# Clustered attention with a gated convolution FFN: the first batch's slots in another order, and every engine's order list written anew

## Chip, cores and metric

The kernel runs on one core of one Trainium2 chip. The metric is the device time of one execution in microseconds (us), median over several runs. The core's engines each work through their own instructions in order: PE multiplies matrices, DVE and POOL do vector work, ACT does activations (exp, relu, tanh, copies), and SP issues transfers; they wait for each other by semaphores.

## The reference

Four batches, 8 heads, 768 tokens, head size 64. Each query and key is assigned to one of 16 centroids of its head; a query sees only the keys of its own cluster. The attention output, 512 wide, goes through an FFN with a depthwise convolution of three taps over the tokens and a sigmoid gate. Cut to what matters:

```python
q_assign = argmax(einsum('bhsd,hcd->bhsc', q_n, c_n), -1)      # the same for k
scores = where(q_assign[..., :, None] == k_assign[..., None, :], q @ k.T / 8, -1e9)
attn = exp(scores - max); attn /= sum(attn) + 1e-9
x = (attn @ v)                      # heads side by side: 4 x 768 x 512
h = maximum(x @ w_in, 0)            # 1024 wide
conv = sum_k conv_w[k] * h shifted by k - 1 tokens
out = (h * sigmoid(conv)) @ w_out   # 4 x 768 x 512, float32
```

## The kernel before

**Tiling.** The heads go in pairs: 4 pairs per batch, 16 pairs in all, numbered g. A pair's queries are cut into two halves of 384. One pair and one half of the queries make a *slot* t: 8 slots per batch, 32 in all. `slot(t)` gives the pair and the half of a slot; for the first batch from the table `SLOTS0`, for the others half by half, pair by pair. In the table before, slots 0 to 3 are the first half of pairs 0 to 3 and slots 4 to 7 their second half.

**One pair is prepared** so: q and k come in by DMA (`L`, `LQ`, `LK`, `LZ`), are transposed on PE (`T`, line 309) and copied from PSUM (`Qa` by ACT, line 315, `Qd` by DVE, line 317), or transposed in blocks on DVE (`Z`, line 298); half precision copies go into `ext` (`CD` on POOL, `CDd` on DVE, `CDa` on ACT, lines 321 and 323). PE multiplies them with the centroids (`A`, line 347), DVE finds the largest in seven steps (`M0` to `M6`, lines 364 to 389). The cluster number is coded into three extra rows of `ext`, so that the product of q and k gets the mask with it: PE turns the codes (`K` and `B`, and `BX` writes the rows by DMA; or `KM` on PE and `KCa`/`KCd` copy them straight from PSUM; `BA` is `BX` on ACT's DMA queue). The rows of `ext` that are not used are zeroed once (`_z` on POOL, `_zd` on DVE, line 716). There are six `ext` buffers.

**One slot** has six steps i: `S.t.i` multiplies two key tiles with the 384 queries (line 442, contracting over all 128 rows of `ext`), `E.t.i` takes the exp of both on ACT (line 454). `V.t.u` multiplies with v (line 466; v loaded by `LV`, cast by `CV`), `N.t` divides by the sums on DVE, and x is transposed into `xT` by PE (`X`, then `Ya`/`Yd`) or by DMA (`XD`).

**The FFN** of a batch works on a half of the tokens: it needs the `xT` of all four pairs of that half. `I.n.f` multiplies with w_in (line 524), `Ra`/`Rd` is the relu (ACT line 537, DVE line 539), `C` carries the tokens at the border between the halves, `a`, `b`, `c` are the three taps on DVE (lines 558, 560) or `W` the same as matmuls on PE, `H` the tanh, `G` the gate on DVE, `O`/`U` multiply with w_out (line 604), `Fa`/`Fd` take the result out of PSUM and `FX` stores it. Weights come in pieces (`_wl`), cast by POOL, DVE or ACT (`_wp`, `_wd`, `_wa`); `_tp`, `_td`, `_ta` build the diagonal matrices of the taps; `_k` runs three matmuls on zeros.

**The order** of all this is written out by hand: `PLAN` is a list of such tokens. They are issued in this order, and each engine, and SP's queue of transfers, keeps the order in which its own instructions come up. Two things share buffers in turn: four input buffers hold the q and k of the pairs and also the pieces of weights (`load_weights` uses the tag `qk_in`), and the PSUM banks, whose number stands behind `@` in a token. A line of the list begins with the exp that opens a slot (`E.t.0`).

Of the kernel before, what the change touches and what calls it, by code (L numbers as in the profile page):

```python
# [155 lines left out]
def kernel(  # L156
# [12 lines left out]
    B, H, S, D = q.shape  # L169
    P = 128  # L170
    J = S // P
    C = 16
# [3 lines left out]
    R = Dm // P  # L176
    HS = S // 2
    VW = D + 2
    NPR = H // 2
    SPB = 2 * NPR  # L180
    NU = 2 * NPR
    BR = 3
    SHARP = 24.0


    CUT = HS - 2
    LO = (0, CUT)
    NCV = (CUT, S - CUT)
# [31 lines left out]
    NE = 6  # L220
# [216 lines left out]
    def scores(t, i):  # L437
        b, a, pr, g = slot(t)
# [433 lines left out]
```

## Time and profile before

| | us |
|---|---|
| median of 3 runs | 241.73 (241.42 to 241.91) |
| the profiled execution, its own time | 240.68 |
| its span | 238.9 |
| matmuls busy (PE) | 227.7 |
| DVE busy | 215.4 |
| ACT busy | 215.4 |
| POOL busy | 84.6 |
| the exps on ACT, 192 of them | 146.4 |

The span is what the hardware profiler records between the first and the last instruction; the execution's own time has what lies around it too. Busy times of engines overlap; a busy PE means that some matmul was in flight. The granted TensorE clock was 0.998 of full speed over the span.

### The profile page before, as it was taken

How to read it: one execution, taken by the hardware profiler on the slowest of the kernel's cores; microseconds unless marked ns; L12 is line 12 of the kernel's file. 1: busy time of each engine (PE TensorE's matmuls, PEld its weight loads, DVE VectorE, ACT ScalarE, POOL GpSimd, SP SyncE). 2: the span in 40 equal slices, each digit the busy share in tenths (PEclk: the TensorE clock that was granted, in tenths of full speed). 3: DMA queues.
4: the chain of work that ended last, by engine and by line, in shares of the span. 5: the costliest groups of instructions: out<-in, count | busy, mean ns of one | idle time of the engine just before them, and what ended most of it. 6: DMA issues, size and time to landing. Idle time of an engine off the chain costs nothing.

```text
span 238.9 us, 6438 instructions
## 1 busy us (share of the span) xinstructions
PE 227.7 (95%) x2442; PEld 143.5 (60%) x2442; DVE 215.4 (90%) x497; ACT 215.4 (90%) x337; POOL 84.6 (35%) x149
## 2 busy tenths in 40 slices
PE   7988998999999999999999999999999999999984
PEld 4665665575556566655666666655776666555531
DVE  6999999989999999999899999999899999983850
ACT  5998997999999999999999999999999999994542
POOL 8559664790168335411935031304540001000000
PEclk9999999999999999999999999999999999999999
DMA  7988599944956975878669507890542110323104
GB/s 198 294 243 257 157 233 245 323 80 83 242 92 136 183 128 94 173 126 183 163 150 169 114 3 188 153 134 1 168 89 63 33 47 16 105 64 112 68 0 177
DMA packets 102958, 32.77 MB, mean 137 GB/s; under 512 B 94603, under 2 KB 98187, under 8 KB 102926
## 3 DMA queue, kind: packets, MB, share of 16 engines
q1 hardware_dynamic: 102599, 32.11, 57.3%
q8 instruction: 19, 0.31, 0.6%
q10 hardware_dynamic: 327, 0.24, 0.4%
q14 instruction: 13, 0.11, 0.1%
HBM read 23.11 MB, written 6.29 MB: 123 GB/s over the span
## 4 chain that ended last, share of the span: by engine, by line
PE 64%; DVE 15%; ACT 12%; POOL 5%; issue 2%; DVEq 0%; POOLq 0%
PE sc L442 17%; PE flex L524 15%; PE flex L604 14%; PE flex L466 10%; ACT attn L454 8%; PE flex L347 3%; POOL ext L323 3%; PE sc L566 3%; ACT th L584 2%; DVE best L380 1%; DVE ext L323 1%; DVE cnv L560 1%; DVE x L480 1%; PE sc L604 1%; DVE val L377 1%
## 5 line engine op out<-in xcount | busy, mean ns | idle before, releaser
L454 ACT ACTIVATE attn<-sc 128x768 f16<-128x768 f32 x192 | 146.4, 817 | 4.0 <-PE sc L442 2.7
L442 PE MATMUL sc<-ext 128*128 128x384 f16 x384 | 89.3, 325 | 3.8 <-ACT attn L454 2.1
L466 PEld LDWEIGHTS <-attn 128*128 128x128 f16 x1152 | 50.5, 97 | 15.2 <-ACT attn L454 0.4
L560 DVE SCALAR_TENSOR_TENSOR cnv<-hpad,cwcol,cnv 128x382 f16<-128x382 f16 (+1 forms) x100 | 58.4, 609 | 0.4
L323 POOL CAST ext<-qkT 64x768 f16<-64x768 f32 x48 | 41.7, 875 | 40.6 <-DVE qkT L298 20.0
L466 PE MATMUL flex<-v,attn 128*128 128x65 f16 x1152 | 54.5, 193 | 0.3 <-ACT attn L454 0.3
L524 PE MATMUL flex<-xT,w_in 128*128 128x384 f16 x256 | 49.1, 326 | 0.1
L442 PEld LDWEIGHTS <-ext 128*128 128x128 f16 x384 | 32.5, 97 | 26.9 <-issue 9.2
L604 PE MATMUL flex<-w_out,hg 128*128 128x512 f16 x176 | 47.1, 379 | 0.0
L592 DVE SCALAR_TENSOR_TENSOR hg<-th,hpad 128x764 f16<-128x764 f32 (+2 forms) x33 | 30.7, 934 | 3.1 <-ACT th L584 3.0
L524 PEld LDWEIGHTS <-w_in 128*128 128x128 f16 x256 | 23.9, 98 | 15.6 <-issue 0.6
L604 PEld LDWEIGHTS <-hg 128*128 128x128 f16 x192 | 17.9, 98 | 16.8 <-DVE hg L592 1.1
L537 ACT ACTIVATE hpad<-flex 128x384 f16<-128x384 f32 x45 | 21.8, 501 | 2.4 <-PE flex L524 1.6
L323 POOL CAST v<-v_in 128x768 f16<-128x768 f32 x15 | 14.6, 977 | 24.7 <-DMA v_in<-in_v_dram 24.6
L584 ACT ACTIVATE th<-cnv 128x764 f32<-128x764 f16 (+1 forms) x25 | 21.2, 848 | 0.7 <-DVE cnv L560 0.7
L323 POOL COPY hpad<-hf 128x6 f16<-128x6 f16 x12 | 4.9, 418 | 42.0 <-DVE hg L592 41.8
L480 DVE TENSOR_TENSOR x<-flex,rec 128x384 f16<-128x384 f32 x32 | 17.8, 558 | 1.1
L298 DVE STREAM_TRANSPOSE qkT<-qk_in 128x768 f32<-128x768 f32 x18 | 17.3, 966 | 0.0
L558 DVE TENSOR_SCALAR cnv<-hpad,cwcol 128x382 f16<-128x382 f16 (+1 forms) x50 | 16.3, 349 | 0.6 <-ACT hpad L537 0.5
L323 POOL COPY hf<-hpad 128x6 f16<-128x6 f16 x11 | 3.6, 329 | 30.7 <-ACT hpad L537 18.6
L347 PE MATMUL flex<-qkT,cT 128*32 128x192 f32 x256 | 14.1, 333 | 0.0
L309 PE MATMUL flex<-id,qk_in 128*128 128x128 f32 x84 | 12.5, 287 | 1.2 <-ACT qkT L315 0.6
(82 smaller groups left out, 217.1 us busy)
## 6 DMA issues: line engine op xcount, KB each, us to landing
v_in<-in_v_dram SPq DMA_DIRECT2D x16, 384.0 KB
out_dram<-o_sb SPq DMA_DIRECT2D x24, 256.0 KB
qk_in<-in_q_dram SPq DMA_DIRECT2D x36, 96.0 KB
qk_in<-in_k_dram SPq DMA_DIRECT2D x36, 96.0 KB
qk_in<-in_q_dram SPq DMA_DIRECT2D x5, 384.0 KB
qk_in<-in_k_dram SPq DMA_DIRECT2D x5, 384.0 KB
w_sb<-in_moe_w_out_dram SPq DMA_DIRECT2D x2, 768.0 KB
w_sb<-in_moe_w_in_dram SPq DMA_DIRECT2D x3, 512.0 KB
```

The lines of the kernel that those rows point to most:

```text
L323: (nc.vector if name == "d" else nc.gpsimd).tensor_copy(out=to, in_=src)
L347: nc.tensor.matmul(bank[at][32 * j : 32 * (j + 1), 192 * i : 192 * (i + 1)], lhsT=cT32[:, which, :], rhs=tokens[:, j], start=True, stop=Tr ...
L442: nc.tensor.matmul(s[:, n, 0:HS], lhsT=ext_b[g % NE][:, h, 1, P * (kt + n) : P * (kt + n + 1)], rhs=ext_b[g % NE][:, h, 0, HS * a : HS * ( ...
L454: nc.scalar.activation(attn[t, i // 3][:, kt : kt + 2, :], sc[(6 * t + i) % 2][:, :, 0:HS], AF.Exp, scale=0.125)
L466: nc.tensor.matmul(avp(at)[:, u, 0 : D + 1], lhsT=attn[t, h][:, kt, P * jq : P * (jq + 1)], rhs=v16_b[g % NE][:, h, kt, 0 : D + 1], start= ...
L480: nc.vector.tensor_tensor(out=x16[t].rearrange("p jq (h d) -> p h jq d", h=2), in0=av[:, :, 0:D].rearrange("p (h jq) d -> p h jq d", h=2), ...
L524: nc.tensor.matmul(bank[at][:, 0:HS], lhsT=w_in16[:, r, 2 * u + f, :], rhs=xT[:, b % 2, r, HS * a : HS * (a + 1)], start=(r == 0), stop=(r ...
L537: nc.scalar.activation(to, src, AF.Relu)
L560: nc.vector.scalar_tensor_tensor(out=cnv, in0=src, scalar=w, in1=cnv, op0=ALU.mult, op1=ALU.add)
L584: nc.scalar.activation(th_t[n][:, fs, 0:N], pre[:, fs, 0:N], AF.Tanh, scale=0.5)
L592: nc.vector.scalar_tensor_tensor(out=hg_b[b][:, 2 * u + fs.start : 2 * u + fs.stop, LO[a] : LO[a] + N], in0=th_t[n][:, fs, 0:N], scalar=1. ...
L604: nc.tensor.matmul(bank[at][:, 0:Dm], lhsT=hg_b[b][:, fb, P * tq : P * (tq + 1)], rhs=w_out16[:, fb, :], start=(fb == 0), stop=(fb == NFB ...
```

## The change

Three edits. The table `SLOTS0` gets another order: slot 0 is the first half of pair 0 as before, slot 1 is the second half of the same pair, and then come the first halves of pairs 1, 2 and 3 and the second halves of pairs 1, 2 and 3. `PLAN` is written anew as a whole: the order of the tokens in all slots, the PSUM banks, and for some small steps the engine that does them (relus, casts, copies, taps, memsets); transfers of bias rows for pair 1, head 1 move from ACT's queue (`BA.1.1`) to SP's (`BX.1.1`); one group of matmuls on zeros (`_k.3`) is left out. The matmuls of the scores name their rows by a constant `KR`, which is 128.

The diff, with the list's first slots and its end:

```diff
-    "LQ.0.0 _id _io _zero _k.10@2 _zd.5.0 _k.17@3 _zd.3.0 _zd.3.1 _pk.4 _sd _z.0.1 _k.14@1 _hz.1 _z.1.1 "
-    "_cent _n1 _z.1.0 _z.0.0 _hz.2 _pk.0 _v.1 _z.2.1 _pk.2 _pk.1 _z.4.0 T.0.0@2 La.0.0 T.0.1@1 _n0 _nq _n2 "
-    "_n5 _id16 _zd.4.1 _n3@3 _n4@3 Qa.0.0 Qa.0.1 CDd.0.0.1 CDa.0.0.0 LK.0.1 T.0.3@2 Qa.0.3 A.0.0@3 M0.0.0 "
-    "M1.0.0 M2.0.0 M3.0.0 _cw0 LQ.0.1 T.0.2@1 Qa.0.2 CDa.0.1.1 LQ.1.0 T.1.0@0 _cw1@2 _cw2 _tp.20 Qa.1.0 "
-    "A.0.1@1 M4.0.0 M0.0.1 M1.0.1 M5.0.0 M2.0.1 M6.0.0 M3.0.1 LK.1.0 T.1.1@3 Qa.1.1 _ta.10 CDd.1.0.0 LQ.1.1 "
-    "T.1.2@1 Qa.1.2 LK.1.1 T.1.3@0 A.1.0@2 M0.1.0 M1.1.0 Qa.1.3 CD.1.1.1 _ta.6 _td.22 KM.0.0.1@1 KCa.0.0.1 "
-    "KM.0.0.0@3 KCd.0.0.0 M4.0.1 M2.1.0 M3.1.0 M4.1.0 A.1.1@2 M0.1.1 M5.1.0 M5.0.1 M6.1.0 M6.0.1 M1.1.1 "
-    "_z.5.1 CDa.0.1.0 S.0.0 "
-    "E.0.0 L.2 T.2.0@0 Qa.2.0 T.2.2@1 Qa.2.2 T.2.1@3 Qa.2.1 CD.2.1.1 CD.1.1.0 CD.1.0.1 S.0.1 E.0.1 _n7d "
...
-    "S.0.3 E.0.3 S.0.4 E.0.4 K.1.1@0 B.1.1 BA.1.1 _ta.7 M4.2 M5.2 M6.2 L.4 T.4.2@3 T.4.0@2 T.4.1@1 S.0.5 "
...
-    "S.4.0 T.6.1@0 Qd.6.1 V.2.5@2 K.5@3 S.4.1 "
...
-    "V.5.5@2 N.5 CD.7.0.1 CD.6.1.0 _wl.1 _wp.4 _wp.3 _wl.2 _wp.6 _v.5 I.0.0@0 Rd.0.0 c.0.0 _wa.7 _wa.5 "
...
+    "_sd _pk.4 _zero _k.10@2 _zd.4.1 _k.17@3 _k.14@3 _pk.3 _id _id16 _z.0.1 _pk.1 _z.0.0 _pk.0 _z.1.0 _io "
+    "_z.2.1 _z.1.1 _v.2 LQ.0.0 T.0.0@3 _cent _n1 _zd.5.1 La.0.0 _n0 _nq _n2 _n3@1 _n5 _n4@1 Qa.0.0 T.0.1@2 "
+    "Qd.0.1 CDd.0.0.1 LK.0.1 T.0.3@0 LQ.0.1 T.0.2@3 Qa.0.2 Qa.0.3 CDa.0.1.0 CD.0.1.1 A.0.0@1 M0.0.0 M1.0.0 "
+    "LQ.1.0 _cw0 _cw1@3 _cw2 _ta.10 _tp.11 A.0.1@2 M2.0.0 LK.1.0 LK.1.1 T.1.3@3 T.1.0@0 _z.3.1 M0.0.1 M3.0.0 "
+    "M1.0.1 M4.0.0 M2.0.1 LQ.1.1 T.1.2@2 Qa.1.0 Qa.1.2 T.1.1@1 Qa.1.1 M5.0.0 M6.0.0 M3.0.1 M4.0.1 KM.0.0.1@2 "
+    "KCd.0.0.1 Qa.1.3 _ta.9 CDa.0.0.0 CD.1.1.1 CD.1.0.0 _z.2.0 _n7d A.1.0@1 M0.1.0 M1.1.0 M2.1.0 KM.0.0.0@3 "
+    "KCa.0.0.0 _ta.23 A.1.1@2 M0.1.1 L.2 T.2.0@0 Qa.2.0 S.0.0 "
+    "E.0.0 S.0.1 T.2.1@3 Qa.2.1 T.2.2@2 Qa.2.2 S.0.2 M3.1.0 M4.1.0 M5.1.0 M5.0.1 M6.0.1 _tp.20 _v.4 M1.1.1 "
+    "M2.1.1 M6.1.0 CD.2.1.1 M3.1.1 M4.1.1 CD.1.1.0 CD.1.0.1 CD.2.0.0 CD.2.0.1 KM.0.1.0@1 K.1.0@3 B.1.0 "
+    "KCd.0.1.0 A.2@2 M0.2 KM.0.1.1@3 KCd.0.1.1 _v.1 M1.2 M2.2 E.0.1 CDa.2.1.0 E.0.2 _ta.19 L.3 T.3.0@0 "
+    "Qa.3.0 T.3.2@2 Qd.3.2 T.3.1@3 Qa.3.1 CD.3.0.1 _v.0 S.0.3 S.0.4 E.0.3 E.0.4 CD.3.1.0 _tp.15 M5.1.1 M3.2 "
+    "M4.2 M5.2 M6.1.1 A.3@2 M0.3 M6.2 CDa.3.1.1 S.0.5 E.0.5 S.1.0 "
+    "E.1.0 M1.3 K.1.1@2 B.1.1 L.4 T.4.2@0 T.4.0@3 Qa.4.0 _ta.4 T.4.1@1 Qd.4.2 Qd.4.1 L.5 LV.0 BX.1.0 S.1.1 "
+    "S.1.2 CD.3.0.0 CV.0 _pk.2 E.1.1 L.6 LV.1 BX.1.1 T.5.0@2 Qa.5.0 M2.3 M3.3 CDd.4.0.1 K.2@0 B.2 LV.2 A.4@3 "
...
+    "S.3.3 K.4@2 S.3.4 V.2.0@1 V.2.1@1 E.3.3 E.3.4 S.3.5 E.3.5 _wl.4 _wd.14 V.2.2@1 V.2.3@1 M2.5 V.2.4@1 "
+    "V.2.5@1 N.2 M3.5 BX.3 S.4.0 _wl.0 LV.3 LZ.7.0 LZ.7.1 S.4.1 "
...
+    "E.5.0 _wd.0 V.3.5@3 N.3 S.5.2 M2.6 V.4.3@1 V.4.4@1 E.5.1 E.5.2 S.5.3 E.5.3 V.4.5@1 X.2@0 Ya.2 N.4 "
+    "V.5.0@2 V.5.1@2 S.5.4 S.5.5 _hz.2 CD.6.0.0 _tp.6 _wp.13 CD.6.1.0 _z.5.0 _wp.12 CD.6.1.1 E.5.4 _ta.8 "
+    "E.5.5 M3.6 M4.6 A.7@3 M0.7 _wd.1 M1.7 S.6.0 V.5.2@2 K.5@0 S.6.1 "
+    "E.6.0 V.5.3@2 V.5.4@2 E.6.1 S.6.2 E.6.2 M5.6 M6.6 CDa.7.1.1 _wl.1 _wl.2 _wd.8 BX.4 X.3@1 K.6@3 B.6 B.5 "
+    "Yd.3 V.5.5@2 N.5 S.6.3 E.6.3 S.6.4 E.6.4 CD.7.0.0 CD.7.0.1 M2.7 _wp.4 _tp.18 _wp.5 _wp.6 XD.4 I.0.1@3 "
+    "I.0.0@2 Rd.0.0 c.0.0 M3.7 Ra.0.1 c.0.1 a.0.0 a.0.1 b.0.0 b.0.1 _wp.3 _wp.7 LV.5 CV.5 S.6.5 E.6.5 "
...
+    "U.3.3.4@5 H.31.0 H.31.1 G.31.0 G.31.1 U.3.3.5@5 U.3.3.6@5 U.3.5.0@3 U.3.3.7@5 U.3.5.1@3 U.3.5.2@3 "
+    "U.3.2.6@4 Fa.3.3 FX.3.3 U.3.5.3@3 U.3.2.7@4 U.3.5.4@3 U.3.5.5@3 U.3.5.6@3 U.3.5.7@3 Fa.3.2 FX.3.2 "
...
+    KR = P
...
-    SLOTS0 = ((0, 0), (0, 1), (0, 2), (0, 3), (1, 0), (1, 1), (1, 2), (1, 3))
+    SLOTS0 = ((0, 0), (1, 0), (0, 1), (0, 2), (0, 3), (1, 1), (1, 2), (1, 3))
...
-                lhsT=ext_b[g % NE][:, h, 1, P * (kt + n) : P * (kt + n + 1)],
-                rhs=ext_b[g % NE][:, h, 0, HS * a : HS * (a + 1)],
+                lhsT=ext_b[g % NE][0:KR, h, 1, P * (kt + n) : P * (kt + n + 1)],
+                rhs=ext_b[g % NE][0:KR, h, 0, HS * a : HS * (a + 1)],
```

232 rows, old and new, of the table PLAN are left out of this document.

## The prediction

> **What bounds the kernel now.** I read the page's totals first, then the windows that cut the span where the stages change, then what ACT waited for, then the order of time around those waits. The first fence is from the page: the span and the busy time of each engine.
>
> ```profile
> span 238.9 us, 6438 instructions
> PE 227.7 (95%) x2442; PEld 143.5 (60%) x2442; DVE 215.4 (90%) x497; ACT 215.4 (90%) x337; POOL 84.6 (35%) x149
> ```
>
> Three engines are at 90% or more, so no single total says which one ends the program. The windows do: busy time of PE, PEld, DVE, ACT and POOL (and how many instructions) before the first exp, from there to the last exp of slot 10, to the end of the last exp, and the tail.
>
> ```profile
> 0.00:13.52 13.52, 10.92 (x90) 7.03 (x91) 11.15 (x32) 10.41 (x20) 9.10 (x36) 1.00 0.94 249
> 13.52:79.22 65.70, 61.64 (x765) 41.18 (x764) 62.69 (x156) 62.41 (x97) 38.35 (x57) 1.00 0.77 190
> 79.22:215.74 136.52, 136.26 (x1477) 85.70 (x1476) 131.55 (x293) 133.23 (x205) 36.95 (x55) 1.00 0.52 108
> 215.74:238.90 23.16, 18.86 (x116) 9.61 (x113) 9.97 (x19) 9.35 (x17) 0.19 (x1) 0.98 0.25 92
> ```
>
> From 79.22 to 215.74 us PE has 0.26 us without a matmul: there PE is the bound, ACT and DVE are close behind, and the same PE work in another order takes about the same time. Between 13.52 and 79.22 us PE lacks 4.06 us, ACT 3.29 us and DVE 3.01 us: no engine is full, they wait for each other. A change to the first batch can win there, and before it in the head, where ACT is idle for 3.11 us.
>
> What ACT waited for between 5 and 80 us (total, times, longest), and those two places in the order of time (start, length, engine, instruction, idle before it):
>
> ```profile
> ACT attn L454 <- PE sc L442: 1.6, 3, 1.2
> ACT taps L745 <- DVE pack L389: 0.9, 1, 0.9
> ```
>
> ```profile
> 21.22 1.37 ACTq L410 DMA_DIRECT2D ext<-spk  x1
> 22.64 0.40 ACT L745 ACTIVATE taps<-id,cwcol 128x128 f16<-128x128 f16 x1 [0.93 <-DVE pack L389]
> ...
> 40.53 0.22 PE L401 MATMUL flex<-id,pack 128*128 128x128 f16 x1 [0.43 <-DVE qkT L317]
> ...
> 41.11 2.41 ACT L454 ACTIVATE attn<-sc 128x768 f16<-128x768 f32 x3 [1.23 <-PE sc L442]
> ```
>
> The first place: ACT stands 0.93 us while its own queue issues the bias rows' DMA of pair 1, head 1 (`BA.1.1`, 1.37 us). The second: in slot 4 the order list puts `K.5@3` ahead of `S.4.1`, so a turn that waits for DVE holds up the scores, and ACT loses 1.23 us.
>
> **The change, part by part.** `KR = P` leaves both operands of the scores as they are: nothing. The slots' order and the lists are the change. With slot 1 on pair 0, pair 1 is first needed in slot 2, pairs 2 and 3 in slots 3 and 4, one slot later than now; the first half's FFN input needs slots 0, 2, 3, 4. Counted in the two lists, every matrix product, exp, argmax, gate and store is there once in both; what differs is who does the small work. Durations are the group means (busy us, then mean ns of one):
>
> ```profile
> L537 ACT ACTIVATE hpad<-flex 128x384 f16<-128x384 f32 x45 | 21.8, 501 | 2.4 <-PE flex L524 1.6 <-DVE hg L592 0.2
> L321 ACT ACTIVATE ext<-flex 3x768 f16<-3x768 f16 x2 | 1.6, 801 | 0.1
> L321 ACT ACTIVATE w_in<-w_sb 128x512 f16<-128x512 f32 x2 | 1.1, 620 | 0.0
> L745 ACT ACTIVATE taps<-id,cwcol 128x128 f16<-128x128 f16 x9 | 3.5, 402 | 0.9 <-DVE pack L389 0.9
> L323 DVE CAST ext<-qkT 64x768 f16<-64x768 f32 x9 | 5.5, 610 | 0.2
> L539 DVE TENSOR_SCALAR hpad<-flex 128x384 f16<-128x384 f32 x19 | 10.4, 549 | 1.7 <-PE flex L524 1.7
> L748 DVE TENSOR_SCALAR taps<-id,cwcol 128x128 f16<-128x128 f16 x5 | 1.6, 321 | 0.0
> L716 DVE MEMSET ext<- 64x768 f32 x4 | 2.8, 698 | 0.6 <-issue 0.4
> L323 POOL CAST ext<-qkT 64x768 f16<-64x768 f32 x48 | 41.7, 875 | 40.6 <-DVE qkT L298 20.0 <-PE sc L442 11.3 <-ACT qkT L315 4.5
> L323 POOL CAST v<-v_in 128x768 f16<-128x768 f32 x15 | 14.6, 977 | 24.7 <-DMA v_in<-in_v_dram 24.6
> L748 POOL TENSOR_SCALAR taps<-id,cwcol 128x128 f16<-128x128 f16 x10 | 6.9, 694 | 1.6 <-DVE cwcol L734 1.1
> L716 POOL MEMSET ext<- 64x768 f32 x8 | 5.7, 733 | 0.3
> ```
>
> DVE: 3 relus fewer (-1.65), 3 casts of ext fewer (-1.83), 4 taps fewer (-1.28), 2 memsets fewer (-1.40): -6.2 us, of which about 1.8 us comes back (two casts of v and one copy of bias rows, priced like ext casts at 0.610). Net -4.3 us, 1.4 of it in the head; single small steps that go either way are left out. POOL takes it: 3 ext casts (+2.63), 5 taps (+3.47), 2 memsets (+1.47), 2 v casts fewer (-1.95): +5.6 us. ACT up to the last exp of slot 10: one copy of bias rows fewer (-0.80), two weight casts fewer (-1.24), one relu more (+0.50), one tap more (+0.40): -1.1 us. PE: three warm-up matmuls fewer in slot 0; they lie in the stage in which PE lacks 4.06 us of work, so they are hidden there and I price them at nothing (if PE were short of time, their going would be a gain).
>
> *Up to slot 10.* ACT has 62.41 of 65.70 us filled, so 1.1 us less work on it shows as 1.1 us: **-1.1** (0 if it only adds idle time; -1.1). `BA.1.1` becomes `BX.1.1` on SP: the 0.93 us stall goes: **-0.9** (0 to -0.93). What it now stands behind is SP's loads. Counted in the list, pairs 0 to 6 and two values, 6.3 MB, go out ahead of it; the head's rate is
>
> ```profile
> DMA packets 9440, 4.16 MB, mean 260 GB/s; under 512 B 8047, under 2 KB 9436, under 8 KB 9439
> ```
>
> so it lands near 6.3 / 0.26 = 24 us or shortly after its own issue, and `S.2.3` wants it only at about 30: hidden, and if not, 1 us for each us it is late. The stall before `S.4.1`: in the new list no turn lies between `S.3.5` and `S.4.1`, but what DVE does late can hold another token. Bounds -1.23 and 0; I take half: **-0.6**.
>
> *The head* pays. These rows are the present chain to the first exp:
>
> ```profile
> 5.48 0.70 DVE L716 MEMSET ext<- 64x768 f32 x1 [0.20 <-issue]
> 6.78 0.53 PE L347 MATMUL flex<-qkT,cT 128*32 128x192 f32 x8
> 7.24 0.87 PE L309 MATMUL flex<-id,qk_in 128*128 128x128 f32 x6
> 11.02 0.83 PE L418 MATMUL flex<-id,pack 128*3 128x128 f16 x12
> 12.38 0.56 DVE L323 COPY ext<-flex 3x768 f16<-3x768 f16 x1
> 13.52 0.81 ACT L454 ACTIVATE attn<-sc 128x768 f16<-128x768 f32 x1 [0.18 <-PE sc L442]
> ```
>
> Now `A.0.0` (6.78) runs ahead of the transposes of head 1 (7.24, three of those six belong to it); in the new list it stands behind them: half of 0.87, +0.4, though it may be less where the data is early. The argmax of head 0 has the same companions on DVE until its last step. Then both bias rows' transposes come as one pack of twelve (11.02); the new list puts `A.1.0` between them and gives the second copy to ACT at 0.80 instead of 0.56 on DVE, behind an ext cast: +0.5. First exp at 14.4 instead of 13.52: **+0.9**. Bounds: -0.2 (the memset at 5.48 that now precedes `n4` moves ahead, and all else hides) and +1.9 (ACT, which in this list stands still for `T.0.2` after its first copy, loses a whole further microsecond).
>
> *The start of the FFN.* `I.0.1` needs all four `w_in` rows cast. The first FFN matmul now, and POOL before it:
>
> ```profile
> L524 PE MATMUL flex<-xT,w_in x256: 323/326/337, 52.1 to 225.9; 128*128 128x384 f16 x128
> 47.67 1.59 POOL L323 CAST ext<-qkT 64x768 f16<-64x768 f32 x2
> 49.21 2.05 POOL L323 CAST w_in<-w_sb 128x512 f16<-128x512 f32 x3
> ```
>
> POOL ends its casts at 51.26 and PE starts at 52.1. In the new list POOL does two ext casts of pair 7 (they wait for `S.5.5`), `_wp.4`, a tap, `_wp.5` and `_wp.6` ahead of `I.0.1`: 2 x 0.82 + 2.05 + 0.69 = 4.4 us after about 47.7, so about 52 again, while the rest of the program would be 1.7 us early. One more pair of score matmuls with its exp now stands ahead of the first FFN matmul, which covers part of it, and ACT and DVE go on meanwhile: **+0.5** (0 to +1.7).
>
> *From slot 11 on:* the same PE work, 0.26 us of holes: 0 (a hole anywhere adds; I allow +-0.7). *Tail:* four more output matmuls are left after the last exp and as many fewer lie before it; PE loses 0.69 us now near the end behind an evacuation, and the new list has one matmul of cover there: 0 (+-0.5).
>
> ```profile
> 232.62 0.59 PE L604 MATMUL sc<-w_out,hg 128*128 128x512 f16 x2 [0.69 <-ACT o_sb L617]
> ```
>
> Sum: +0.9 -1.1 -0.9 -0.6 +0.5 = **-1.2 us**. The profiled execution took 240.68 us by its own clock (span 238.9), 1.05 us less than the median of the runs, 241.73; the difference is applied to the median: 240.5 us.
>
> **Rivals.** (a) *Hidden anyway.* The microsecond won by slot 10 is lost again because ACT and DVE, at 133.23 and 131.55 of 136.52 us, can't follow a PE that arrives earlier: 241.7, within 0.2% (0.48 us, about what can be told from no change here). For: DVE and ACT together leave under 9 us in that stretch; against: their work there is hardly changed.
>
> (b) *The other side: POOL holds up the FFN.* Slot 5 in the new list carries two POOL tap/memset steps, two `w_out` casts and three ext casts where the old one has nothing on POOL, and the buffer of `_wl.2` is free only after the last `w_out` cast; behind `_wl.2` on SP stand `BX.4` and `XD.4`, both needed soon. If POOL hasn't run ahead, `_wp.6` is late by up to the 5.6 us that POOL gained; I take half, 2.8 us, against the 1.7 us that the earlier steps win: +1.1, 242.8. It decides once the first FFN matmul starts later than 52.1 + 1.7 = 53.8 us.
>
> (c) *DVE and POOL disturb each other.* Small DVE steps vary widely (min/median/max ns):
>
> ```profile
> L389 DVE SCALAR_TENSOR_TENSOR pack<-best,pack x32: 128/164/823, 10.4 to 173.3; 128x12 f16<-128x12 f32 x32
> L558 DVE TENSOR_SCALAR cnv<-hpad,cwcol x50: 307/316/880, 54.4 to 225.1; 128x382 f16<-128x382 f16 x26, 128x386 f16<-128x386 f16 x24
> ```
>
> The 823 against a median of 164 is a step held for about one POOL cast (0.82 us). The new lists have eight POOL instructions more net of what goes; if each held a DVE step 0.66 us, DVE would pay 5.3 us and have no saving left (-4.3 + 5.3 = +1.0), and with the head and the FFN start as above 1.0 + 0.9 + 0.5 gives +2.4: 244.1. By what these two lines show, most steps are at the median, and the eight cost a few tenths.
> [...]
>
> (d) *More is won.* Head and FFN start cost nothing and both ACT stalls go: -1.1 -0.9 -1.2 = -3.2: 238.5.
>
> **How the numbers follow.** Forecast 0.45 (240.5; its own range 239.5 to 241.2); (d) 0.10; (a) 0.15; (b) 0.23; (c) 0.07. Faster by over 0.2%: 0.45 + 0.10 = 0.55, less 0.02 for the forecast's edge near no change, 0.53. Same: 0.15 + 0.02 = 0.17. Slower: 0.23 + 0.07 = 0.30. Leaving out (c) and the outer half of (d), the range runs from 238.7 to 243.3; its upper end lies 0.5 over (b) for the unknown holes after slot 11.
>
> **What would show it.** Right: first exp at about 14.4 us; no ACT DMA at 21 us; the last exp of slot 10 ends near 78; the first FFN matmul at 52 or before; PE holes after slot 10 as small as now; DVE busy about 4 us less, POOL nearly 6 more. Wrong: a first exp after 15.5, a first FFN matmul after 53.8, DVE's short steps on average longer than now, or PE holes of more than a microsecond between slots 11 and 31.

## The result, and the profile after

The changed kernel takes 243.75 us (median of 20 executions, 241.85 to 248.55) against 241.09 us for the kernel before on the same chips (20 executions, 240.33 to 244.48): a ratio of 1.0083, 95% interval 1.0061 to 1.0105. It is slower by 0.8%; I had forecast 240.5 us and given "faster" 0.53. In eight of the twenty executions, the profiled one among them (247.07 us), the granted clock of TensorE over the span is 0.979 or 0.986 and the time 246.7 to 248.6 us, in the other twelve it is 0.993 to 1.000 and 241.9 to 244.1 us, and the ratio leaves out the eight, and of the kernel before those that lie over 1.5% above its fastest.

The page of the changed kernel: span, busy time of each engine, and the granted clock in 40 slices.

```profile
span 245.3 us, 6420 instructions
...
PE 228.9 (93%) x2439; PEld 144.3 (59%) x2439; DVE 219.9 (90%) x488; ACT 215.1 (88%) x338; POOL 90.6 (37%) x157
...
PEclk9999799998999999999999999999999999999999
```

POOL has 6.0 us more to do (counted: 5.6). DVE has nine instructions less and yet is busy 4.5 us longer. The clock falls twice, in slices 5 and 10. The stretches from the first exp to the last exp of slot 10, to the last exp of all, and the tail (length; busy time and number of instructions of PE, PEld, DVE, ACT and POOL; clock; DMA):

```profile
13.63:87.07 73.44, 63.65 (x758) 42.17 (x757) 68.16 (x147) 63.00 (x96) 44.31 (x73) 0.95 0.69 171
87.07:222.44 135.37, 135.30 (x1475) 85.13 (x1474) 131.24 (x293) 132.84 (x206) 35.08 (x50) 1.00 0.50 110
222.44:245.30 22.86, 18.52 (x115) 9.72 (x113) 9.58 (x18) 9.25 (x19) 0.46 (x1) 1.00 0.22 82
```

The head costs 0.1 us (first exp at 13.63, before 13.52), the long stretch and the tail are 1.15 and 0.30 us shorter than before (136.52 and 23.16). All of the loss lies in the first batch: 73.44 us where it was 65.70. The clock fell in it too; e2 below shows the same stretch at full clock. There PE waited for (total, times, longest):

```profile
PE flex L402 <- DVE sim L365: 2.7, 1, 2.7
PE flex L402 <- DVE pack L390: 2.2, 1, 2.2
PE flex L402 <- DVE qkT L318: 2.1, 1, 2.1
PE flex L348 <- DVE pack L387: 1.1, 1, 1.1
```

Three times a turn of cluster codes (`K.1.1`, `K.6`, `K.4`) stands at the head of PE's queue and waits for DVE. In order of time (start, length, engine, instruction, idle before it) at the first and the last of the three:

```profile
21.72 1.50 DVE L387 TENSOR_SCALAR pack<-best 128x24 f16<-128x24 f32 x1
23.13 0.84 DVE L390 SCALAR_TENSOR_TENSOR pack<-best,pack 128x12 f16<-128x12 f32 x1
...
54.20 1.73 DVE L378 TENSOR_TENSOR val<-eqq,iota 128x384 f16<-128x384 f16 x1
```

```profile
21.02 0.82 POOL L324 CAST ext<-qkT 64x768 f16<-64x768 f32 x1
21.81 0.60 POOL L749 TENSOR_SCALAR taps<-id,cwcol 128x128 f16<-128x128 f16 x1
22.37 0.82 POOL L324 CAST ext<-qkT 64x768 f16<-64x768 f32 x1
23.13 0.82 POOL L324 CAST v<-v_in 128x768 f16<-128x768 f32 x1
...
53.36 2.36 POOL L324 CAST w_in<-w_sb 128x512 f16<-128x512 f32 x4
```

```profile
24.52 0.22 PE L402 MATMUL flex<-id,pack 128*128 128x128 f16 x1 [2.66 <-DVE sim L365]
24.58 2.39 PE L310 MATMUL flex<-id,qk_in 128*128 128x128 f32 x12
```

The same steps in the kernel before, grouped over its first 55 us:

```profile
L377 DVE TENSOR_TENSOR val<-eqq,iota 128x384 f16<-128x384 f16 x6 | 2.5, 412 | 0.1
L386 DVE TENSOR_SCALAR pack<-best 128x24 f16<-128x24 f32 x4 | 1.0, 244 | 0.1
```

The `pack` step (`M5`), there 0.24 us on average, takes 1.50 us: it starts while POOL works and ends at 23.22 us, when three POOL instructions on end are through (22.37 + 0.82 = 23.19). The next step, `M6`, meets a fourth. At 54.20 `val` does the same behind four casts. And right behind the first PE gap the clock is halved: 0.50 from 25.0 to 28.4 us.

```profile
20.00:25.00 5.00, 2.09 (x25) 1.38 (x26) 4.93 (x11) 2.97 (x4) 4.08 (x11) 1.00 0.58 179
25.00:28.40 3.40, 3.40 (x16) 2.72 (x15) 2.24 (x6) 1.75 (x3) 0.57 (x1) 0.50 0.33 87
```

DVE is busy 4.93 of the 5.00 us before that: it isn't waiting for anyone, and it gets through only 11 instructions (m5 below, in the same 5 us: 4.90 us busy with 13). So the first theory ("hold", in the expectations also "port"): POOL's runs of instructions hold DVE's short steps, PE waits for those, and a halved clock follows the gap. Rivals: the list puts the turns too early ("turns"); the new order prepares the pairs too late, whoever does the work ("order"); the clock falls for want of matmuls on zeros ("clock").

### The profile page after: what moved, and what is told of

Its sections match the earlier page's. It is cut to its first block, busy times and chain, and to the rows that moved or that the text cites. A ratio compares the mean times of both kernels' runs of the same rounds, so it can differ in the third digit from the quotient of the medians.

```text
span 245.3 us, 6420 instructions
## 1 busy us (share of the span) xinstructions
PE 228.9 (93%) x2439; PEld 144.3 (59%) x2439; DVE 219.9 (90%) x488; ACT 215.1 (88%) x338; POOL 90.6 (37%) x157
## 4 chain that ended last, share of the span: by engine, by line
PE 73%; DVE 13%; ACT 4%; DMA 3%; POOL 3%; issue 2%; SPq 0%; DVEq 0%; ACTq 0%
PE sc L443 20%; PE flex L525 16%; PE flex L605 15%; PE flex L467 12%; ACT attn L455 3%; PE flex L348 3%; PE sc L567 2%; DMA qk_in<-in_k_dram 2%; PE flex L310 2%; PE sc L605 1%; DVE val L378 1%; DVE qkT L318 1%; DVE sim L365 1%; DVE cnv L561 1%; POOL ext L324 1%
## 5 line engine op out<-in xcount | busy, mean ns | idle before, releaser
L443 PE MATMUL sc<-ext 128*128 128x384 f16 x384 | 91.4, 328 | 1.1 <-ACT attn L455 0.4
L324 POOL CAST ext<-qkT 64x768 f16<-64x768 f32 x51 | 44.2, 870 | 53.1 <-PE sc L443 17.0
L467 PEld LDWEIGHTS <-attn 128*128 128x128 f16 x1152 | 48.9, 97 | 14.0 <-DVE x L481 0.6
L467 PE MATMUL flex<-v,attn 128*128 128x65 f16 x1152 | 52.2, 193 | 0.2 <-DVE x L481 0.2
L525 PE MATMUL flex<-xT,w_in 128*128 128x384 f16 x256 | 50.4, 333 | 0.0
L525 PEld LDWEIGHTS <-w_in 128*128 128x128 f16 x256 | 25.0, 99 | 17.8 <-issue 2.0
L538 ACT ACTIVATE hpad<-flex 128x384 f16<-128x384 f32 x48 | 24.0, 504 | 4.4 <-PE flex L525 3.0
L324 POOL CAST v<-v_in 128x768 f16<-128x768 f32 x13 | 12.7, 975 | 22.0 <-DMA v_in<-in_v_dram 16.8
L310 PE MATMUL flex<-id,qk_in 128*128 128x128 f32 x84 | 13.4, 298 | 0.1
L316 ACT ACTIVATE qkT<-flex 128x512 f32<-128x512 f32 (+1 forms) x16 | 8.3, 555 | 5.5 <-PE flex L310 4.6
```

What stands on the lines that cost most here:

```text
L310: nc.tensor.transpose(bank[at][:, P * i : P * (i + 1)], blocks, id128[:])
L324: (nc.vector if name == "d" else nc.gpsimd).tensor_copy(out=to, in_=src)
L443: nc.tensor.matmul(s[:, n, 0:HS], lhsT=ext_b[g % NE][0:KR, h, 1, P * (kt + n) : P * (kt + n + 1)], rhs=ext_b[g % NE][0:KR, h, 0, HS * a : ...
L467: nc.tensor.matmul(avp(at)[:, u, 0 : D + 1], lhsT=attn[t, h][:, kt, P * jq : P * (jq + 1)], rhs=v16_b[g % NE][:, h, kt, 0 : D + 1], start= ...
L525: nc.tensor.matmul(bank[at][:, 0:HS], lhsT=w_in16[:, r, 2 * u + f, :], rhs=xT[:, b % 2, r, HS * a : HS * (a + 1)], start=(r == 0), stop=(r ...
L538: nc.scalar.activation(to, src, AF.Relu)
```

## The experiments

The kernels that follow have the order list in fewer lines, so their line numbers are 15 lower: L387 of the changed kernel is L372 there. "Slot 5 at +2.6" means that the last exp of slot 5 ends 2.6 us later than in the profile of the kernel before (49.68 us).

**e1: the three turns later.** In the changed kernel `K.1.1`, `K.4` and `K.6` go behind the next scores.

```diff
-E.1.0 M1.3 K.1.1@2 B.1.1 L.4 ... S.1.1 S.1.2
+E.1.0 M1.3 L.4 ... S.1.1 S.1.2 K.1.1@2 B.1.1
```

> The changed kernel with three turns of bias codes later in PE's order: K.1.1 and its copy behind S.1.2, K.4 behind S.3.5, K.6 and its copy behind S.6.4. Nothing else moves. Theory 'turns' (PE stands behind turns whose argmax is late on DVE, while ready transposes and scores queue behind them: 2.66 us at 21.9, 2.10 us at 40.2, 2.19 us at 56.0): the three PE gaps shrink under 0.7 us each, the kernel gains 2 to 4 us on the changed one and comes to a ratio of 0.995 to 1.002 to the kernel before. Theory 'port' (DVE itself is late because POOL holds it, and everything needs DVE): the gaps only move to the next thing that waits for DVE; gain under 1 us, ratio 1.005 to 1.009.

245.47 us, ratio 1.0139 (1.0099 to 1.0179). That is worse than either theory expected. The gaps only move (0.70 us at 24.1 and 1.70 us at 25.0), the clock is halved for 6.8 us from 26.2. The turns aren't placed too early; what they wait for is late. "Turns" falls.

**e2: nine more matmuls on zeros** ahead of `K.1.1`.

```diff
-K.1.1@2 B.1.1
+_k.3@0 _k.14@0 _k.17@0 K.1.1@2 B.1.1
```

> The changed kernel with nine matmuls on zeros put ahead of K.1.1, in the place where PE stood 2.66 us. Theory 'clock' (the stretches of 3.4 us at half clock after 25 and 59 us follow from PE's idle time, and they are what some executions lose): the first half-clock stretch goes, the profiled span loses 1.5 to 2 us against the changed kernel's slow executions and the undisturbed ones stay at 1.006 to 1.010 of the kernel before. If idle time on PE does not set the clock: the half-clock stretch near 25 us is still there.

243.09 us, ratio 1.0076 (1.0047 to 1.0104). The profiled execution has no halved clock ahead of the last exp and still slot 3 at +3.5 and slot 5 at +2.6. From the first exp to the last exp of slot 10:

```profile
13.64:81.54 67.90, 61.84 (x767) 41.26 (x765) 65.80 (x146) 62.64 (x96) 44.12 (x73) 1.00 0.74 185
```

That is 2.20 us longer than in the kernel before (65.70), with DVE busy 3.11 us longer (62.69) at ten instructions fewer. So the loss comes without the clock; with the clock halved twice, in the changed kernel's profile, the stretch is 7.74 us longer than before.

**e3: POOL relieved.** Six of POOL's taps go to just ahead of slot 10, three weight casts to ACT.

```diff
-_tp.20 ... _tp.15 ... _tp.13 ... _tp.21 ... _tp.22 ... _wp.4 _tp.18 _wp.5 _wp.6 ... _wp.3 _wp.7
+_wp.4 _wa.5 _wp.6 ... _wa.3 _wa.7 ... _tp.20 _tp.15 _tp.13 _tp.21 _tp.22 _tp.18 E.10.0
```

> The changed kernel with POOL relieved where DVE does the argmax: six diagonal matrices of the taps (20, 15, 13, 21, 22, 18) are built on POOL only ahead of slot 10, and three casts of w_in (3, 5, 7) go to ACT as in the kernel before (5 and 7). Order of PE and DVE unchanged. Theory 'port': DVE's short steps (val, pack, eqq) before 62 us get nearer to the kernel before (val from 1080 ns towards 412 ns, pack from 685 ns towards 244 ns), the turns wait less, gain 1 to 3 us, ratio 0.998 to 1.005. Theory 'turns': DVE's lateness is in the order, the gain is under 0.5 us, ratio 1.006 to 1.010.

244.23 us, ratio 1.0123 (1.0096 to 1.015). Slot 5 comes from +2.6 (e2) to +1.0, but at the new place the six stand ahead of POOL's carries for the convolution, DVE waits 2.42 us for a carry, and PE has a gap of 1.8 us at 83.7: slot 11 at +3.9. So the ratio lies outside both expectations. The place was ill chosen; e5 puts it right.

**e4: the new table of slots alone**, in the old list; the transfer of x of slot 4 (`XD.4`) has to come earlier and went directly behind `N.4`.

```diff
-SLOTS0 = ((0, 0), (0, 1), (0, 2), (0, 3), (1, 0), (1, 1), (1, 2), (1, 3))
+SLOTS0 = ((0, 0), (1, 0), (0, 1), (0, 2), (0, 3), (1, 1), (1, 2), (1, 3))
```

> The kernel before, its list unchanged but for one transfer (XD.4, now the first half of pair 3, moves up behind N.4), with the new order of slots. If the order of slots itself costs: ratio 1.003 to 1.008. If it is neutral and the loss is in the new lists: 0.997 to 1.002. If what I forecast from it is there (pair 1 needed a slot later): 0.993 to 0.998, and the 0.8 us that PE stands at 23.0 us is gone.

251.79 us, ratio 1.0401 (1.0359 to 1.0443), outside all three expectations, and no answer: `XD.4` waited on SP ahead of the loads of weights, POOL cast them late, and the first FFN matmuls stood 5.8 us.

**e5: as e3 with zeros, the taps where POOL stands idle**: four behind the last tap of slot 12, two ahead of slot 16.

```diff
+E.12.0 E.12.1 _tp.5 _tp.20 _tp.21 _tp.22 _tp.18 ... _tp.15 _tp.13 E.16.0
```

> The changed kernel with the nine extra matmuls on zeros of the run before (so that the clock stays up), with the same six taps taken off POOL ahead of slot 10, but issued later, where POOL stood idle: four behind the last tap of slot 12, two ahead of slot 16; and three weight casts on ACT instead of POOL. Theory 'port' (runs of POOL instructions hold DVE's short steps): the last exp of slot 5 ends within 0.9 us of the old kernel's (the changed kernel with warm matmuls: +2.6), nothing is lost at slot 11, ratio to the old kernel 0.998 to 1.004. Theory 'order' (the pairs' preparation is queued less well, whoever does it): slot 5 +2.0 or more, ratio 1.006 to 1.010.

241.24 us, ratio 0.9991 (0.9967 to 1.0015); slot 5 at +0.7. As "hold" has it: the loss is made good, with the same slots and the same order of everything else (three weight casts are on ACT here too; m5 leaves them).

**e6 and e7: engines against order.** e6 is the changed order with the old engines for 80 small steps, e7 the old order with the new engines.

> The changed kernel's slots and order, but each small step (relu, cast, copy, tap, memset, bias rows) on the engine that did it in the old kernel: 80 steps go back. Theory 'port': DVE gets back 4 us of work and POOL loses 6; the val and pack steps of the argmax return to 0.41 and 0.24 us, the last exp of slot 5 within 1 us of the old kernel's, ratio 0.998 to 1.004. Theory 'order': slot 5 at +2.5 or later, ratio 1.006 to 1.015, since the order is the same and DVE and ACT have more to do.

> The old kernel's slots and order with the changed kernel's choice of engines: the same 80 steps the other way. Theory 'port': POOL's runs hold DVE in the old order too: slot 5 ends 1 to 2.5 us later than in the old kernel, ratio 1.004 to 1.012. Theory 'order': less work on DVE and ACT shows as a gain: slot 5 0 to 1.1 us earlier, ratio 0.995 to 1.001.

257.89 us (1.0653, 1.0594 to 1.0712) and 259.18 us (1.0703, 1.0652 to 1.0753): both theories missed by far. Either list with the other's engines runs dry in the first batch (e7: PE waits 5.7 us at 23.1, for the DMA of a q). The choice of engine and the order belong together; which of the 80 do this wasn't tried, and about the hold the two say nothing.

**e8: the slots alone, mended**: as e4, with `XD.4` directly ahead of `I.0.0`, behind the loads.

> The old list and engines with the new order of slots alone; the transfer of x of slot 4 stands directly ahead of the first FFN matmul, behind the loads of weights (in the earlier run of this kind it stood ahead of them and they waited). Theory 'port': the slot order by itself costs nothing up to slot 5 (within 0.7 us), and the first FFN matmul waits for that transfer up to 3 us: ratio 1.000 to 1.010. Theory 'order': slot 1 runs dry because pair 1 isn't wanted yet but everything else stands as before, slots 2 to 5 end 2 us or more later and the FFN another 3: ratio 1.010 to 1.025.

242.78 us, ratio 1.0062 (1.0028 to 1.0096). Slots 0 to 3 end within 0.04 us of before, slot 5 at -0.65: the order of the slots by itself costs nothing there and takes away half of the stall before `S.4.1`. Then the FFN waits for the late transfer, slot 7 at +1.3, and it stays so:

```profile
53.22 0.97 PE L509 MATMUL flex<-xT,w_in 128*128 128x384 f16 x5 [1.16 <-DMA xT<-x]
```

**e9 and e10: e5 taken apart.** e9 leaves out the zeros, e10 keeps them and leaves the weight casts on POOL.

> The run before last's relief (six taps issued late, three weight casts on ACT) on the changed kernel, without the nine extra matmuls on zeros. It separates the two parts of that version. Theory 'clock is a follower' (a stretch at half clock comes only where PE already stood idle because DVE was late): the PE gap behind slot 0 stays under 1.5 us, no stretch at half clock in the profile, ratio 0.998 to 1.004. Theory 'clock is a cause of its own' (without matmuls on zeros the clock falls anyway): half clock for 3.4 us near 25 us, ratio 1.004 to 1.012.

> The changed kernel with the extra matmuls on zeros and only the six taps issued late; the three weight casts stay on POOL. Theory 'port': the taps held DVE in slots 0 to 3, so nearly all is back already: slot 5 ends within 1.0 us of the old kernel's, ratio 0.999 to 1.004. Rival 'POOL's weight casts hold up the FFN': slots 0 to 5 as in the version with both, but the first FFN matmul 1 us or more later than there and ratio 1.004 to 1.008.

e9: 241.2 us, 1.0003 (0.9979 to 1.0026), PE gap 1.3 us, no halved clock: without the zeros and without the long gap the clock stays up, so here it follows, it doesn't lead. e10: 240.38 us, 0.994 (0.9908 to 0.9971): better than both kernels and than "hold" expected, though slot 5 is at +1.3 and the first FFN matmul comes at 55.07, 1.5 us later than in e5 (53.52), as the rival had it. So the taps are enough; whether the casts given to ACT cost what e5 lacked, the intervals of e5 and e10, which overlap, don't tell.

**e11 and e12: the same in the old kernel.** e11 issues its five early POOL taps late; e12 makes six taps twice, where POOL stands idle.

```diff
-_tp.20 ... _tp.19 ... _tp.21 ... _tp.2 ... _tp.13
+CV.7 _tp.20 _tp.19 _tp.21 ... _tp.15 _tp.2 ... _tp.12 _tp.13
```

```diff
-CD.5.0.0
+CD.5.0.0 _tp.20 _tp.20 _tp.20 _tp.20
...
-_tp.13
+_tp.13 _tp.13 _tp.13
```

> The old kernel with its own early POOL taps (five of them) issued late, three behind a cast of v in slot 12, two behind the taps of slots 22 and 25; nothing else changed. Theory 'port': the old kernel pays for its POOL taps too; its val and pack steps get shorter and slots 1 to 5 end 0.3 to 1.0 us earlier, ratio 0.995 to 0.999. Rival (it was only the changed kernel's list that had no slack): 0.999 to 1.002.

> The old kernel with six POOL taps made a second time, placed where POOL stood idle, so that no cast on POOL is late for them: four behind the cast that ended at 28.85 us (POOL idle to 31.64), two behind the one at 39.0 us (idle to 41.47). Theory 'port': DVE's five casts and copies of 0.42 to 0.56 us between 28.9 and 31.6 us are held, some to 0.8 us or more; slots 3 to 5 end 0.5 to 2.0 us later, ratio 1.002 to 1.008. Rival 'lateness of POOL's own casts' (DVE isn't held; the moved taps only let POOL's casts come earlier): DVE's durations as before, slots 3 to 5 within 0.3 us, ratio 0.999 to 1.001.

e11 went against "hold" as I had put it: 244.73 us, 1.011 (1.0069 to 1.0151), slower with less on POOL. Its order of time on DVE, POOL and PE shows why:

```profile
22.71 1.67 DVE L374 SCALAR_TENSOR_TENSOR pack<-best,pack 128x12 f16<-128x12 f32 x2
```

```profile
21.82 1.70 POOL L308 CAST ext<-qkT 64x768 f16<-64x768 f32 x2
```

```profile
25.63 0.22 PE L386 MATMUL flex<-id,pack 128*128 128x128 f16 x1 [0.97 <-DVE qkT L302]
```

Without the taps POOL's two casts come 1.5 us earlier (21.82; before 23.32) and now meet the two `M6` steps, which took 0.35 us together and take 1.67; behind it the clock is halved from 26.0 to 29.4 us, slot 1 at +2.8. So in this run it isn't the amount of POOL's work that counts, but whether a run of it meets and holds a short step that PE waits for. e12: 242.0 us, 1.0015 (0.9977 to 1.0053), undecided as a time; in the profile the DVE casts beside the four taps take 0.57, 0.64, 0.50 and 0.62 us (before 0.55, 0.55, 0.42, 0.56), slot 5 at +0.4. "Hold" had expected 0.8 us or more and a delay of 0.5 to 2.0 us, and that didn't come: four taps on end hold these casts by less than 0.1 us each.

**m1: the hold by itself.** Behind the end of the old kernel DVE runs its kinds of steps three times, each behind a copy out of PSUM, alone and then beside 24 POOL casts back to back. (A part beside taps is missing: by a dependency they came only when DVE was through.)

> The old kernel with a measurement behind its end (its time is not to be compared): DVE goes three times through a cast of 128x512, the val product, a reduction, the pack step and the comparison, each behind a copy out of PSUM; first alone, then beside 24 POOL casts of 64x768 back to back, then beside 32 POOL taps of 128x128; before that POOL works alone. Theory 'hold': alone each DVE step takes its usual time (cast 0.55, val 0.31, reduction 0.54, pack 0.17, comparison 0.54 us); beside POOL the steps that read and write SBUF in short time are held for at least the rest of one POOL instruction, so that pack and val take 0.6 to 1.5 us, while copies out of PSUM and reductions keep their time. If the hold lasts for a run of POOL instructions, single steps reach over 1.7 us. Rival 'coincidence': no step is longer than 1.2 times its time alone.

DVE's groups alone (busy us, mean ns), then beside the casts:

```profile
L861 DVE COPY w_out<-flex 128x512 f32<-128x512 f32 x15 | 10.3, 685 | 0.0
L872 DVE TENSOR_TENSOR w_in<-xT 128x384 f16<-128x384 f32 x3 | 1.6, 549 | 0.0
L868 DVE TENSOR_REDUCE mb<-w_in 128x24 f32<-128x384 f16 x3 | 1.6, 541 | 0.0
L870 DVE TENSOR_SCALAR w_in<-xT 128x24 f16<-128x24 f32 x3 | 0.5, 169 | 0.0
```

```profile
L861 DVE COPY w_out<-flex 128x512 f32<-128x512 f32 x15 | 10.2, 677 | 0.0
L870 DVE TENSOR_SCALAR w_in<-xT 128x24 f16<-128x24 f32 x3 | 2.0, 679 | 0.0
L872 DVE TENSOR_TENSOR w_in<-xT 128x384 f16<-128x384 f32 x3 | 1.9, 634 | 0.0
L868 DVE TENSOR_REDUCE mb<-w_in 128x24 f32<-128x384 f16 x3 | 1.6, 536 | 0.0
```

`pack` (L870) goes from 169 to 679 ns, four times as long, all three times; the comparison gains 85 ns; copies out of PSUM (677 against 685 ns) and reductions (536 against 541) gain nothing. `val` and the cast, 1.73 and 1.50 us long beside POOL casts in the changed kernel (at 54.20 and 50.86 us), gain 39 ns and nothing clear here (one cast, beside POOL casts ahead of the measurement, took 1.02 us): each step comes three times, 5.27 us apart, so few meetings were tried, and no step reached 1.7 us, as the theory wanted it for a hold that lasts through a run. The hold is shown; its length by kind isn't.

The traces of the kernels themselves say more. Over all profiles but that of m1, 183 `pack` steps (128x24) began while POOL stood idle, and none took over 0.18 us; 83 began while a POOL instruction ran, and 52 of these took over 0.24 us, up to 1.51. For `val` (128x384) it is none of 115 (at most 0.36 us) and 55 of 151 (over 0.49 us, up to 1.73). In the profiles of the kernel before and of the changed one, copies of 128x512 out of PSUM take 0.67 to 0.69 us either way, reductions of 128x384 0.51 to 0.55 us and block transposes of 128x768 0.93 to 0.97 us. So in these profiles a short step is held only beside POOL, but not each time: in m5 below a `val` takes 0.35 us in the midst of five POOL casts on end, and of 36 that began beside a POOL tap none took over 0.45 us. What decides among such meetings stays open.

```profile
50.43 0.35 DVE L363 TENSOR_TENSOR val<-eqq,iota 128x384 f16<-128x384 f16 x1
```

```profile
49.87 3.32 POOL L309 CAST w_in<-w_sb 128x512 f16<-128x512 f32 x5 [0.47 <-DMA w_sb<-in_moe_w_in_dram]
```

**m2 and m3: the zeros.** m2 is e11 with nine more matmuls on zeros, m3 the old kernel without the three that the change leaves out (`_k.3@0`).

> The old kernel with its early POOL taps late (the run that was slower, 1.011; half clock from 26.0 to 29.4 us) and nine matmuls on zeros put ahead of the turn of pair 1, head 1. If the halved clock is the larger part of that loss: no stretch at half clock, slot 1 ends 0.5 to 1.3 us late instead of 2.76, ratio 1.002 to 1.005. If the hold on DVE (pack, 1.67 us at 22.7) is the larger part: slot 1 still 2 us late, ratio 1.008 to 1.011.

> The old kernel without the three matmuls on zeros in slot 0 that the change leaves out. As I priced it (hidden): ratio 0.998 to 1.002 and no new stretch at half clock. If these three keep the clock up: half clock for 3.4 us near 25 us in a part of the executions, ratio 1.003 to 1.012.

m2: 242.57 us, 1.0073 (1.0036 to 1.0109), between the two expectations. In its profile the full clock came only at 13.5 us, and the first exp is 2.5 us late; counted from there, slot 5 is 1.1 us late without a halved clock behind slot 0, in e11 2.8 with it: about two fifths hold, the rest clock, by my estimate from one execution each (1.1 of 2.8 us). m3: 241.43 us, 1.0007 (0.9984 to 1.0029): the zeros were worth nothing, as priced.

**m4: e10 less the six tap matrices 12 to 17**, which no matmul reads.

> The changed kernel with nine more matmuls on zeros and four POOL taps issued late (0.994), now also without the six tap matrices 12 to 17 that no matmul reads (four on POOL, two on ACT in slot 31). Theory 'hold, and ACT's tail': as before or 0.3 us better by two ACT steps of 0.4 us in the tail: ratio 0.991 to 0.996. If the good result was chance of alignment, moving the late POOL steps changes nothing up to slot 15, and the ratio goes back to 0.997 to 1.001 all the same.

240.45 us, 0.9972 (0.9952 to 0.9991). That is just above what "hold" expected (0.991 to 0.996) and just inside what I had put down for a chance of alignment (0.997 to 1.001); beside e10 (0.9908 to 0.9971) it is no difference that the intervals tell, so this run decides nothing between the two.

**m5 and m6: one edit each.** m5 only moves the six taps in the changed kernel; m6 leaves them where they are and gives them to DVE.

```diff
-_tp.20 ... _tp.15 ... _tp.13 ... _tp.21 ... _tp.22 ... _tp.18
+_td.20 ... _td.15 ... _td.13 ... _td.21 ... _td.22 ... _td.18
```

> The changed kernel with one edit alone: the six POOL taps of slots 0 to 6 issued in slots 12 and 16, no extra matmuls on zeros, weight casts as they were. Theory 'hold' with the halved clock as its follower: DVE's 38 instructions up to the end of slot 1 take 15.6 us as in the version with zeros, no stretch at half clock, ratio 0.992 to 0.999. If the zeros were needed: half clock behind slot 0, ratio 1.003 to 1.010.

> The changed kernel with the same six taps in their old places, but made by DVE instead of POOL: DVE gets 6 x 0.32 = 1.9 us of work in the stage in which it is always busy, POOL loses 6 x 0.66 = 4 us. Theory 'hold': DVE gets back what the taps held, about 1.7 us by the windows of the two versions, so the two cancel within the halves of the clock: ratio 1.000 to 1.008. Theory 'the list is simply short of DVE time' (POOL does DVE no harm): 1.9 us on top of the changed kernel, ratio 1.013 to 1.020.

m5: 240.86 us, 0.9957 (0.9926 to 0.9989). m6: 240.66 us, 0.9958 (0.9931 to 0.9984), better than "hold" expected. The slowest of their executions (241.63 and 241.49 us) lie below the fastest of the changed kernel (241.85). Six taps on POOL are the whole difference between 0.8% slower and 0.4% faster, and they do no harm where they are, only on that engine. The stages of m5, and the first one of m6:

```profile
14.33:80.54 66.21, 60.53 (x758) 40.39 (x757) 63.50 (x147) 62.67 (x96) 40.61 (x66) 1.00 0.76 185
80.54:216.15 135.61, 135.54 (x1475) 85.02 (x1474) 131.70 (x293) 132.94 (x206) 40.69 (x56) 1.00 0.51 112
216.15:239.10 22.95, 18.53 (x115) 9.70 (x113) 9.58 (x18) 9.25 (x19) 0.46 (x1) 0.96 0.22 81
```

```profile
14.06:80.77 66.71, 60.46 (x758) 40.48 (x756) 65.27 (x153) 62.63 (x96) 40.27 (x66) 1.00 0.73 185
```

Beside the changed kernel's 73.44 us, m5 has the same 147 DVE instructions in 63.50 instead of 68.16 us. Of the 7.23 us, 3.12 are PE's own (63.65 - 60.53: matmuls at half clock) and 4.11 waiting. In m6 DVE does six taps more and is still 2.89 us shorter than in the changed kernel. Against e2, which has the taps and the full clock, m5 is 1.69 us shorter in this stretch (67.90), and its DVE 2.30 us (65.80). The groups of the changed kernel, then of m5, in that stage:

```profile
L378 DVE TENSOR_TENSOR val<-eqq,iota 128x384 f16<-128x384 f16 x7 | 6.1, 869 | 0.1
...
L387 DVE TENSOR_SCALAR pack<-best 128x24 f16<-128x24 f32 x6 | 3.6, 599 | 0.1
L324 DVE CAST w_in<-w_sb 128x512 f16<-128x512 f32 x3 | 2.3, 754 | 0.0
```

```profile
L363 DVE TENSOR_TENSOR val<-eqq,iota 128x384 f16<-128x384 f16 x7 | 4.8, 689 | 0.1
...
L372 DVE TENSOR_SCALAR pack<-best 128x24 f16<-128x24 f32 x6 | 2.3, 386 | 0.1
L309 DVE CAST w_in<-w_sb 128x512 f16<-128x512 f32 x3 | 1.1, 380 | 0.0
```

And the place at which it began, on DVE and on PE in m5:

```profile
22.35 0.92 DVE L372 TENSOR_SCALAR pack<-best 128x24 f16<-128x24 f32 x1
23.18 0.16 DVE L375 SCALAR_TENSOR_TENSOR pack<-best,pack 128x12 f16<-128x12 f32 x1
```

```profile
23.88 0.22 PE L387 MATMUL flex<-id,pack 128*128 128x128 f16 x1 [1.39 <-DVE sim L350]
23.94 1.48 PE L295 MATMUL flex<-id,qk_in 128*128 128x128 f32 x12
```

Without the tap at 21.81 POOL's run is one instruction shorter; the two steps take 0.92 + 0.16 instead of 1.50 + 0.84 us, 1.26 less; counted from the first exp the turn comes 1.34 us earlier (9.55 instead of 10.89), PE's gap is 1.39 instead of 2.66, the clock stays up, and the same twelve transposes take 1.48 us, not 2.39.

## Why the prediction was wrong

**The step that failed** is the price of work moved from DVE to POOL. I booked it as "Net -4.3 us" on DVE and took it that DVE's other steps keep their length: the sum has no term for them, and of rival (c) I wrote that "most steps are at the median, and the eight cost a few tenths". Measured: DVE 4.5 us busier, and at full clock (e2) 2.5 us busier:

```profile
PE 227.2 (95%) x2448; PEld 143.1 (60%) x2448; DVE 217.9 (91%) x488; ACT 214.9 (90%) x338; POOL 91.8 (38%) x157
PE 226.5 (95%) x2439; PEld 142.4 (60%) x2439; DVE 215.8 (90%) x488; ACT 214.9 (90%) x338; POOL 92.3 (39%) x157
```

The second line is m5: even without the six taps DVE is busy 0.4 us longer than before, not 4.3 us less. The groups of DVE steps whose number changed give -4.3 us there, as counted; those whose number stayed take 3.6 us more (e2: -2.5 and +3.9; the changed kernel: -2.8 and +6.6). In kind that is rival (c), and the size that it gave (244.1; measured 243.75) was near, at a chance of 0.07, but not for its reason: it isn't eight instructions with 0.66 us each. A few meetings of a POOL run with a step that PE waits for (0.24 us become 1.50, 0.41 become 1.73) make gaps of 2.66 and 2.19 us. I had quoted the very rows that show it, 823 against 164 ns, and read them as rare; I hadn't asked which of the short steps stand ahead of a PE instruction, nor how long a run of POOL instructions can get. Second, nowhere did I ask what a PE gap of over 2 us does to the clock; in this profile 3.12 us.

The other steps, by the changed kernel and by m5, which is the change without the six taps:
- *Head, +0.9*: first exp at 13.63, 14.33 (m5) and 14.06 (m6), so +0.1 to +0.8 with the same instructions; inside the bounds.
- *ACT's less work, -1.1*: both weight casts and one of the copies of bias rows are gone, as counted, and the lengths of ACT's instructions from the first exp to the last exp of slot 10 add up to 1.15 us less in m5 (70.87, before 72.02). But they overlap less: ACT is busy 62.67 us there, before 62.41, so nothing of the term shows as time. *`BA.1.1` off ACT's queue, -0.9*: no DMA stands there any more, but PE waits for DVE before the same turn (1.39 us in m5), and ACT 1.35 us behind it: a stall that took the place of the one removed.
- *Stall before `S.4.1`, -0.6*: e8, with the new slots in the old list, shows -0.65. In m5 ACT's waits of over 0.15 us in this stretch add up to 2.78 us, before to 2.82: on balance neither of the two stalls was won there.
- *FFN start, +0.5*: first FFN matmul at 59.11, in m5 at 54.26, later than the 53.8 us from which rival (b) was to decide; and yet m5 is faster, since more of the scores now lies ahead of it (slot 6 at +0.2). The sign that I named for (b) was a bad one. *POOL holds up the FFN* wasn't the cause: e10 and m5 leave all its casts on POOL.
- *From slot 11 on, 0*: 135.37 against 136.52, -1.15, with two PE instructions fewer in that stretch; better than my bounds (m5: -0.91). *Tail, 0*: -0.3 (m5: -0.2).
- *Zeros at nothing*: right (m3; and e10 with them, m5 without, agree within their intervals).

So the sum of -1.2 us isn't what m5 does either. By stages its profile stands at +0.8 (head), +0.5 (to the last exp of slot 10), -0.9 and -0.2 us against the kernel before, where the sum had +0.9, -2.1, 0 and 0: only the head was right. That m5, m6 and e10 come out at ratios of 0.994 to 0.996, near the forecast's 0.995, is in part luck. Their medians are 0.4 to 1.0 us under those of the kernel before beside them, and their profiled executions (240.91, 240.66, 241.37 us) take about as long as the one of the kernel before (240.68); where the small gain lies isn't shown. What is shown is that the six taps on POOL turn it into a loss.

## What to carry to other kernels

Moving small work to an idle engine wasn't free here, where that engine held another's steps (six taps on POOL, 1.0083; without them, 0.9957): look not at busy totals but at which short step the bound engine waits for, and keep runs of the neighbour's instructions away from it. When busy time rises on an engine that was given less to do, compare the mean of the same group in both profiles, and ask whether the longer steps began beside a neighbour's instruction. And since one such meeting decided e11 (0.35 us became 1.67, ratio 1.011), judge an order by measuring it, and after each edit read again what the first waits end on.

## What was not expected of the hardware

- A PE gap of 2.66 or 2.19 us, with light matmul work around it, was followed by 3.413 us at a granted clock of 0.50 (24.98 to 28.39 and 59.11 to 62.53 us), 3.1 us of PE time in all; the gap of 2.10 us at 40.2 was not; e1 had 6.83 us on end, and e11 3.413 us behind gaps of 1.22 and 0.97 us. With a gap of 1.39 us (m5) the profile shows none.
- In the changed kernel's profile the clock first rises at 4.50 us and changes next at 6, 7, 16 and 17 times 3.413 us behind that; in that of the kernel before it rises at 5.86 us and falls once, 68 times 3.413 us later (237.96 us, in the tail). So I cut each profile, from the clock's first rise on, into stretches of 3.413 us. Up to the last exp, the profiles of all these kernels have 1225 of them at full clock, by my count (61 each in the kernel before and the changed one). Behind eight the clock fell, and in these PE, by the profile's matmul times, was busy 8 to 44% of the time; behind the other 1217, all with 46% or more, it didn't. (In the changed kernel's tail it didn't fall behind one of 41%, 240.02 to 243.43 us.) The three stretches around the changed kernel's gaps have 22, 46 and 36%, and it fell behind the first and the third:

```profile
21.57:24.98 3.41, 0.75 (x7) 0.55 (x6) 3.38 (x7) 1.51 (x2) 2.55 (x7) 1.00 0.41 143
38.63:42.05 3.42, 1.58 (x20) 1.02 (x19) 2.53 (x6) 2.49 (x4) 2.25 (x5) 1.00 1.14 217
55.70:59.11 3.41, 1.22 (x16) 0.79 (x14) 3.34 (x13) 1.92 (x4) 0.02 (x1) 1.00 0.72 198
```

- By this cut the same gap can fall into one stretch or be split between two, and the first rise, and with it the cut, differs from profile to profile (4.5 us in the changed kernel, 5.4 in m5). That the place of the cut decides whether an order of work loses its clock is my guess; no run tests it.
- The clock's first rise in the head varies: at 5.9 us in the kernel before, 13.5 us in the profile of m2, where the first exp came at 16.05 us. In e4 and m1, which begin as the kernel before does, it came at 13.4 and 13.6 us, and the first exp at 16.08 and 16.20; no run shows why.
- DVE steps beginning beside POOL lasted through several POOL instructions on end (`pack` 1.50 us and `val` 1.73 us in the changed kernel, two `pack` steps 1.67 us in e11), while copies out of PSUM that began beside POOL kept their 0.67 to 0.69 us.
